# Pooled attention and a GELU layer on one core: the first batch in pairs, the loads in another order

## The chip, the cores and the metric

The kernel runs on one core of one Trainium2 chip. The metric is the device time of one execution in microseconds. One execution was also profiled; its span runs from the first to the last instruction that the profile shows, and its own time is a little longer than that.

A core has five engines that run side by side, each through its own list of instructions in order: PE (matmuls and transposes, with PEld for its weight loads), DVE (VectorE), ACT (ScalarE), POOL (GpSimd) and SP, which here only issues DMAs. DMAs are issued from the queues of SP, ACT and POOL and carried by 16 DMA engines. PE writes its results to PSUM, which has eight banks of 512 fp32 numbers for each of 128 partitions.

## The reference

Eight batches of 576 tokens go through attention over pooled keys and values (eight heads of 64), and then all 4608 tokens through two dense layers with a GELU (tanh form) between them.

```python
batch, n_heads, seq, head_dim = (8, 8, 576, 64)
Sp = S // 8                                     # 72 pooled positions
k_p = k.reshape(B, H, Sp, 8, D).mean(axis=3)
v_p = v.reshape(B, H, Sp, 8, D).mean(axis=3)
scores = scale * np.matmul(q, k_p.transpose(0, 1, 3, 2))
attn = softmax(scores)
attn_out = np.matmul(attn, v_p)
x = attn_out.transpose(0, 2, 1, 3).reshape(B * S, H * D)     # 4608 x 512
h = x @ w_in                                    # 512 -> 2048
g = gelu_tanh(h)
out = g @ w_out                                 # 2048 -> 512
```

All inputs and the output are fp32 in HBM.

## The kernel before

The 4608 tokens are worked through in nine groups of 512 (`for g in range(NG)`). A group runs the first layer (16 blocks `fo` of 128 features, four matmuls `ko` each, line 282), a GELU of each block on ACT (line 288), and the second layer (four row blocks, 16 matmuls each, line 291). The attention of batch g + 1 is interleaved by hand with group g. In the first layer, after the GELU of the blocks that the table `plan` names, stand the sums that pool k and v (`k_steps`, `v_steps`, on DVE) and the transposes of k and q on PE. Between the matmuls of the second layer, at the places in `pos`, stand for each of eight units (half a sequence `c`, a pair of heads `pr`): QK (line 211), Exp (line 218), AV (line 231) with the row sums beside it, Ln and Exp for the reciprocal (lines 244 to 249), and the multiply into `xT` (line 257). The order on every engine is the order in which the program issues it (`manual_schedule`); the framework only adds the waits.

Batch 0 has no group before it, so its attention stands alone at the start. Its k is loaded in two halves by SP and ACT, with the last 64 rows behind ACT's half; its v on SP's queue in four parts; its q in two halves on POOL's queue, behind which stand w_in in four column blocks of 512, batch 1's k and q, and w_out in four row blocks. DMAs on POOL's queue also change fp32 into bf16. k is summed on DVE in three adds, transposed into one PSUM bank (line 172), and copied out of it by DVE for the even heads and by ACT for the odd ones (line 178). Idle matmuls (`spin`, line 312) stand where PE would otherwise wait. Batch 0's eight units of scores come first, then v's sums, then eight times AV, Ln, Exp and the multiply, one unit at a time, with 16 of the first layer's matmuls for the first 288 tokens put between the last units. Batch 1's v is loaded by SP's queue after the fourth of these units: a memset on DVE (line 344) holds the load back until then.

What sets the order of batch 0's later units:

```python
for i, (c, pr) in enumerate(ORDER):
    bank = (4, 6, 0, 2, 4, 6, 4, 6)[i]
    av(0, c, pr, bank)
    norm(0, c, pr, bank)
    mult(0, c, pr, bank)
    if i == 3:
        vs[1] = kvp.tile([Sp, H, 512], F32, name="vt")
        nc.vector.memset(vs[1][:, 0, 0:1], 0.0)
        load_v(1, nc.sync)
```

and what of batch 1 stands in group 0's first layer:

```python
plan = {0: kk, 4: tk, 6: tq[:1], 7: tq[1:2], 8: tq[2:3], 9: tq[3:], 10: v0, 12: v1}
```

In group 0's second layer the first 32 matmuls take both of two row blocks through four features at a time, so that a quarter of w_out is needed every eight matmuls. `load_q`, `load_k` and `load_v` of batch g + 2 are issued at the start of group g, q's transpose by DMA among them.

Of the kernel before, what the change touches and what calls it, by code (L numbers as in the profile page):

```python
# [8 lines left out]
F32 = mybir.dt.float32  # L9
# [9 lines left out]
def kernel(  # L19
# [9 lines left out]
    nc = tc.nc  # L29
# [35 lines left out]
    def load_k(b, engs):  # L65
        rows = k[b].rearrange("h (j l) d -> (h j) (l d)", l=8)
        main = rows[0:128 * KR].rearrange("(p r) c -> p r c", r=KR)
        n = KR // len(engs)
        for i, eng in enumerate(engs):
            eng.dma_start(out=kts[b % 2][:, i * n:(i + 1) * n], in_=main[:, i * n:(i + 1) * n])  # L70
        engs[-1].dma_start(out=kts[b % 2][64:128, KR], in_=rows[128 * KR:])

    def load_v(b, eng, h0=0, h1=H):
        if b not in vs:
            vs[b] = kvp.tile([Sp, H, 512], F32, name="vt")
        rows = v[b, h0:h1].rearrange("h (j l) d -> j h (l d)", l=8)

        for j0, j1 in ((0, 64), (64, Sp)) if eng is nc.sync else ((0, Sp),):
            eng.dma_start(out=vs[b][j0:j1, h0:h1], in_=rows[j0:j1])
# [8 lines left out]
    w_in_b = consts.tile([128, KO, DF], BF16, name="w_in_b")  # L88
    w_out_b = consts.tile([128, FO, DM], BF16, name="w_out_b")
    w_in_v = moe_w_in.rearrange("(ko p) f -> p ko f", p=128)  # L90
    w_out_v = moe_w_out.rearrange("(fo p) d -> p fo d", p=128)
# [4 lines left out]
    load_v(0, nc.sync, 0, 4)  # L96
    load_v(0, nc.sync, 4, 8)
# [4 lines left out]
    def load_w_in(i):  # L102
        nc.gpsimd.dma_start(out=w_in_b[:, :, i * 512:(i + 1) * 512], in_=w_in_v[:, :, i * 512:(i + 1) * 512])  # L103

    load_w_in(0)
    load_w_in(1)
# [21 lines left out]
    nc.gpsimd.memset(kTs[1], 0.0)  # L128
    nc.gpsimd.memset(kps[1], 0.0)
    nc.gpsimd.memset(kts[1][0:64, KR], 0.0)  # L130
    nc.gpsimd.memset(vps[0], 8.0)  # L131
    nc.gpsimd.memset(vps[1], 8.0)  # L132

    load_k(1, [nc.gpsimd])
    load_q(1)
    load_w_in(2)
    load_w_in(3)
    for i in range(4):
        nc.gpsimd.dma_start(out=w_out_b[:, 4 * i:4 * i + 4, :], in_=w_out_v[:, 4 * i:4 * i + 4, :])

# [3 lines left out]
    def add(o, a, b):  # L144
        nc.vector.tensor_tensor(out=o, in0=a, in1=b, op=ALU.add)  # L145

    def k_steps(b):

        t = kts[b % 2]
        return [lambda: add(t[:, :, 0:256], t[:, :, 0:256], t[:, :, 256:512]),  # L150
                lambda: add(t[:, :, 0:128], t[:, :, 0:128], t[:, :, 128:256]),
                lambda: add(kps[b % 2][:, 0:KR + 1], t[:, :, 0:64], t[:, :, 64:128])]
# [15 lines left out]
    def trans_k(b, bank, odd_eng=None):  # L168
        tp = half_bank(bank)[:, 0:(KR + 1) * 128].rearrange("p (r c) -> p r c", c=128)
        kf = kps[b % 2].rearrange("p r d -> p (r d)")  # L170
        for r in range(KR + 1):
            nc.tensor.transpose(out=tp[:, r, :], in_=kf[:, r * D:r * D + 128], identity=identb)  # L172
        tp = tp[0:D]
        n7 = (H - 1) * KH
        for e in range(2):
            copy = nc.scalar.copy if e and odd_eng is nc.scalar else nc.vector.tensor_copy
            o = kTs[b % 2][e * 64:(e + 1) * 64, e]
            copy(out=o[:, 0:H - 1].rearrange("p h (j r) -> p h j r", r=KR),  # L178
                 in_=tp[:, 0:KR, 0:n7].rearrange("p r (h j) -> p h j r", j=KH))
            copy(out=o[:, H - 1, 0:(128 - n7) * KR].rearrange("p (j r) -> p j r", r=KR),  # L180
                 in_=tp[:, 0:KR, n7:128].rearrange("p r j -> p j r"))
            copy(out=o[:, H - 1, (128 - n7) * KR:], in_=tp[:, KR, 64:128])

    def trans_q(b, i, t0, n, bank, eng):
        if b not in qTs:
            qTs[b] = bp.tile([128, 2, TP, 128], BF16, name="qT")
        tp = half_bank(bank)[:, 0:n * 128].rearrange("p (t c) -> p t c", c=128)
        for x in range(n):
            nc.tensor.transpose(out=half_bank(bank)[:, x * 128:(x + 1) * 128],
                                in_=qs[b][:, i, (t0 + x) * 128:(t0 + x + 1) * 128],  # L190
                                identity=identb)
        o = qTs[b][:, i, t0:t0 + n]
        if eng is nc.scalar:
            nc.scalar.copy(out=o, in_=tp)
        else:
            nc.vector.tensor_copy(out=o, in_=tp)

# [43 lines left out]
    def norm(b, c, pr, bank):  # L241
        ld = ep.tile([128, CH], F32, name="ld")
        if b:
            nc.scalar.activation(out=ld[0:64], in_=PS[64:128, bank, :CH], func=ACT.Ln)  # L244
            nc.scalar.activation(out=ld[64:128], in_=PS[0:64, bank + 1, :CH], func=ACT.Ln)  # L245
        else:
            nc.scalar.activation(out=ld, in_=PS[:, bank + 1, :CH], func=ACT.Ln)
        rc = ep.tile([128, CH], F32, name="rc")
        nc.scalar.activation(out=rc, in_=ld, func=ACT.Exp, scale=-1.0)  # L249
        rcs[b, c, pr] = rc  # L250

    def mult(b, c, pr, bank):
        rc = rcs.pop((b, c, pr))
        col = b * S + c * CH
        for x in range(2 if b else 1):
            rows = slice(x * 64, (x + 1) * 64) if b else slice(0, 128)
            nc.vector.tensor_tensor(out=xT[rows, pr, col:col + CH], in0=PS[rows, bank + x, :CH],  # L257
                                    in1=rc[rows], op=ALU.mult)

# [20 lines left out]
    def p1_mm(g, fo, ko, c0=0, c1=GROUP):  # L280
        r0 = g * GROUP
        nc.tensor.matmul(out=PS[:, h_bank(g, fo), c0:c1], lhsT=w_in_b[:, ko, fo * 128:(fo + 1) * 128],  # L282
                         rhs=xT[:, ko, r0 + c0:r0 + c1], start=(ko == 0), stop=(ko == KO - 1))
# [20 lines left out]

    act_set(EXP_SET)
    for s in k_steps(0):
        s()

    def spin(n):

        for _ in range(n):
            nc.tensor.matmul(out=PS[:, 7, :], lhsT=idle[:, 0:128], rhs=idle, start=True, stop=True)  # L312

    def scores(b, c, pr, bank):
        qk(b, c, pr, bank)
        expo(b, c, pr, bank)

    spin(16)
    trans_q(0, *QG[0], 5, nc.scalar)
    trans_q(0, *QG[1], 6, nc.scalar)  # L320
    spin(4)
    trans_k(0, 4, nc.scalar)
    trans_q(0, *QG[2], 5, nc.vector)
    trans_q(0, *QG[3], 6, nc.vector)
    spin(2)
    for i, (c, pr) in enumerate(((0, 0), (0, 1), (1, 0), (1, 1), (0, 2), (0, 3), (1, 2), (1, 3))):
        if i:
            spin(1)
        scores(0, c, pr, (2, 0)[i % 2])
    for hf in range(2):  # L330
        for s in v_steps(0, hf):
            s()

    early = [(fo, ko) for ko in range(KO) for fo in range(4)]
    take = (0, 0, 0, 0, 0, 4, 6, 6)
    for i, (c, pr) in enumerate(ORDER):
        bank = (4, 6, 0, 2, 4, 6, 4, 6)[i]
        av(0, c, pr, bank)
        norm(0, c, pr, bank)
        mult(0, c, pr, bank)  # L340
        if i == 3:

            vs[1] = kvp.tile([Sp, H, 512], F32, name="vt")
            nc.vector.memset(vs[1][:, 0, 0:1], 0.0)
            load_v(1, nc.sync)
        for fo, ko in early[:take[i]]:
            p1_mm(0, fo, ko, 0, CH)
        early = early[take[i]:]


    for g in range(NG):
        nb = g + 1 if g + 1 < B else None
        act_set(GELU_SET)
        if g + 2 < B:

            load_q(g + 2)
            trans_q_dma(g + 2)
            nc.gpsimd.tensor_copy(out=gate, in_=qTs[g + 2][0:1, 1, TP - 1, 0:2])  # L358
            load_k(g + 2, [nc.gpsimd])
            load_v(g + 2, nc.gpsimd)  # L360


        side = {fo: [] for fo in range(FO)}
        if nb is not None:
            kk = k_steps(nb)
            v0, v1 = v_steps(nb, 0), v_steps(nb, 1)
            tk = [lambda: trans_k(nb, 4)]
            if g:
                plan = {2: kk[:1], 3: kk[1:], 7: v0[:1], 8: v0[1:], 9: tk, 11: v1[:1], 12: v1[1:]}
            else:  # L370
                tq = [lambda a=a, i=i: trans_q(nb, *a, 4 + i, nc.vector) for i, a in enumerate(QG)]
                plan = {0: kk, 4: tk, 6: tq[:1], 7: tq[1:2], 8: tq[2:3], 9: tq[3:], 10: v0, 12: v1}
            for fo, what in plan.items():
                side[fo] += what
# [3 lines left out]
        if g == 0:  # L378
            first = [(fo, ko, CH) for ko in range(KO) for fo in range(4)]
        else:  # L380
            late = 3
            rest = [fo for fo in range(4) if fo != late]
            first = [(fo, ko, 0) for ko in range(2) for fo in rest]
            first += [(late, 0, 0), (late, 1, 0)]
            first += [(fo, ko, 0) for ko in (2, 3) for fo in rest + [late]]
        for fo, ko, c0 in first:
            p1_mm(g, fo, ko, c0)
        for fo in range(FO):
# [4 lines left out]
            for s in side[fo]:  # L393
                s()

# [63 lines left out]
```

The softmax here doesn't subtract the row's maximum and nothing guards it: scores larger than these inputs give would overflow.

## Time and profile before

| | us |
|---|---|
| median of 3 runs | 312.05 (310.88 to 312.41) |
| the profiled execution | 311.66 |
| its span | 309.9 |
| PE busy | 296.7 (96% of the span) |
| ACT busy | 220.9 (71%) |
| DVE busy | 157.1 (51%) |
| POOL busy | 30.8 (10%) |

Busy times are sums over the span and PE's include idle matmuls. The profile also has the span in 40 slices of 7.75 us, the chain of waits that ended last, groups of instructions with the mean time of one, a timeline, and the DMA queues with their packets; each can be asked for a stretch of time. "idle before <-releaser" is the time that an engine stood still ahead of an instruction, and what ended it.

### The profile page before, as it was taken

The numbers are of one execution on the slowest core, as the hardware profiler recorded it, in microseconds if no ns is written. First come the engines' busy times: TensorE is split into PE (matmuls) and PEld (weight loads), VectorE is DVE, ScalarE is ACT, GpSimd is POOL, SyncE is SP. The second block draws the span as 40 slices with busy tenths as digits, with TensorE's granted clock in tenths as the row PEclk, the third lists the DMA queues.
The fourth block names the chain that finished last, engine by engine and source line by source line (L and its number), as shares of the span: only waits on it lengthen the run. The fifth ranks groups of instructions, "written<-read, shape, count | busy, mean of one in ns | idle before, by whom it ended". The sixth has DMA issues, their size and how long they took to land.

```text
span 309.9 us, 4249 instructions
## 1 busy us (share of the span) xinstructions
PE 296.7 (96%) x1516; PEld 149.5 (48%) x1545; DVE 157.1 (51%) x304; ACT 220.9 (71%) x414; POOL 30.8 (10%) x54
## 2 busy tenths in 40 slices
PE   7788899999999999999999999999999999999994
PEld 2455455444544455445544554455445544444441
DVE  3867536647568455855495358636772640020011
ACT  1597478877997799778987898689868987306500
POOL 8530000300301200030003000200000000000000
PEclk9999999999999999999999999999999999999999
DMA  7999995894895982588358826572101120121022
GB/s 225 232 279 249 178 200 116 266 225 87 258 224 113 237 186 62 112 225 175 85 110 232 185 68 100 166 182 68 41 0 33 49 56 0 36 68 34 2 68 69
DMA packets 32701, 41.05 MB, mean 132 GB/s; under 512 B 17608, under 2 KB 21704, under 8 KB 31784
## 3 DMA queue, kind: packets, MB, share of 16 engines
q0 software_dynamic: 10160, 24.26, 35.4%
q1 hardware_dynamic: 22200, 15.74, 21.8%
q10 hardware_dynamic: 320, 0.79, 0.8%
q8 instruction: 12, 0.20, 0.3%
q14 instruction: 9, 0.07, 0.1%
HBM read 36.70 MB, written 9.44 MB: 149 GB/s over the span
## 4 chain that ended last, share of the span: by engine, by line
PE 83%; DMA 12%; POOL 2%; issue 1%; ACT 0%; DVE 0%; POOLq 0%
PE PS L291 38%; PE PS L282 36%; DMA w_out_b<-in_moe_w_out_dram 8%; DMA kt<-in_k_dram 4%; PE PS L211 4%; PE PS L231 4%; PE PS L172 1%; POOL w_in_b L103 0%; POOL kT L128 0%; POOL qb L84 0%; POOL vp L131 0%; POOL vp L132 0%; DVE osb L296 0%; ACT e L218 0%; POOL kt L130 0%
## 5 line engine op out<-in xcount | busy, mean ns | idle before, releaser
L291 PE MATMUL PS<-w_out_b,gT 128*128 128x512 bf16 x560 | 133.8, 379 | 0.9
L282 PE MATMUL PS<-xT,w_in_b 128*128 128x512 bf16 (+2 forms) x580 | 128.3, 373 | 1.8 <-DMA w_in_b<-in_moe_w_in_dram 0.9
L288 ACT ACTIVATE gT<-PS 128x512 bf16<-128x512 f32 x144 | 81.3, 603 | 48.4 <-PE PS L282 48.2
L282 PEld LDWEIGHTS <-w_in_b 128*128 128x128 bf16 x592 | 57.2, 98 | 66.4 <-issue 2.0
L291 PEld LDWEIGHTS <-gT 128*128 128x128 bf16 x576 | 56.0, 97 | 57.1 <-issue 0.8
L296 DVE COPY osb<-PS 128x512 f32<-128x512 f32 x36 | 24.9, 692 | 94.9 <-PE PS L291 94.9
L257 DVE TENSOR_TENSOR xT<-PS,rc 64x288 bf16<-64x288 f32 (+1 forms) x120 | 54.6, 455 | 29.9 <-ACT rc L249 22.3
L218 ACT ACTIVATE e<-PS 72x576 bf16<-72x576 f32 x64 | 40.7, 644 | 8.4 <-PE PS L211 7.6
L145 DVE TENSOR_TENSOR vt<-vt 72x1024 f32<-72x1024 f32 (+1 forms) x32 | 30.5, 952 | 7.0 <-DMA vt<-in_v_dram 6.2
L249 ACT ACTIVATE rc<-ld 128x288 f32<-128x288 f32 x64 | 28.3, 443 | 2.1
L211 PE MATMUL PS<-qT,kT 128*72 128x288 bf16 x128 | 26.1, 286 | 0.4 <-ACT e L218 0.3
L244 ACT ACTIVATE ld<-PS 64x288 f32<-64x288 f32 x56 | 22.8, 408 | 1.4
L245 ACT ACTIVATE ld<-PS 64x288 f32<-64x288 f32 x56 | 22.5, 402 | 1.4
L263 ACT ACT_TABLE_LOAD x17 | 21.8, 1283 | 2.1 <-issue 1.8
L231 PE MATMUL PS<-e,vp 72*128 72x288 bf16 x112 | 23.1, 285 | 0.0
L211 PEld LDWEIGHTS <-kT 128*72 128x72 bf16 x128 | 14.4, 113 | 14.2 <-issue 1.4
L145 DVE TENSOR_TENSOR kt<-kt 128x1280 f32<-128x1280 f32 (+1 forms) x16 | 18.5, 1158 | 4.7 <-DMA kt<-in_k_dram 4.3
L358 POOL COPY gate<-qT 1x2 bf16<-1x2 bf16 x6 | 1.1, 176 | 155.8 <-DMA qT<-qb 155.8
L178 DVE COPY kT<-PS 64x504 bf16<-64x504 bf16 x15 | 10.1, 675 | 7.1 <-PE PS L172 7.0
L231 PEld LDWEIGHTS <-vp 72*128 72x128 bf16 x112 | 11.0, 98 | 3.3
L312 PE MATMUL PS<-idle 128*128 128x512 bf16 x28 | 9.6, 467 | 1.2 <-DVE idle L120 1.2
L145 DVE TENSOR_TENSOR vp<-vt 72x128 bf16<-72x128 f32 x28 | 6.9, 284 | 0.6
(45 smaller groups left out, 75.5 us busy)
## 6 DMA issues: line engine op xcount, KB each, us to landing
out_dram<-osb SPq DMA_DIRECT2D x142, 64.0 KB, 1.7
kt<-in_k_dram POOLq DMA_DIRECT2D x7, 1024.0 KB, 5.8
vt<-in_v_dram POOLq DMA_DIRECT2D x6, 1152.0 KB, 12.4
qb<-in_q_dram POOLq DMA_DIRECT2D x7, 576.0 KB, 15.1
w_in_b<-in_moe_w_in_dram POOLq DMA_DIRECT2D x4, 512.0 KB, 18.4
w_out_b<-in_moe_w_out_dram POOLq DMA_DIRECT2D x4, 512.0 KB, 25.0
vt<-in_v_dram SPq DMA_DIRECT2D x2, 512.0 KB, 11.1
vt<-in_v_dram SPq DMA_DIRECT2D x1, 1024.0 KB, 11.6
```

What stands on the lines that cost most here:

```text
L145: nc.vector.tensor_tensor(out=o, in0=a, in1=b, op=ALU.add)
L211: nc.tensor.matmul(out=PS[:Sp, bank + e, :CH].rearrange("j (t p) -> j t p", p=32), lhsT=kTs[b % 2][:, c, h, :], rhs=qTs[b][:, h // 4, :, h ...
L218: nc.scalar.activation(out=e, in_=PS[:Sp, bank:bank + 2, :CH], func=ACT.Exp, scale=1.0 / 64.0)
L231: nc.tensor.matmul(out=PS[:, bank + x, :CH], lhsT=flat(vps[b % 2][:, pr, x]), rhs=e[:, x, :], start=True, stop=True)
L244: nc.scalar.activation(out=ld[0:64], in_=PS[64:128, bank, :CH], func=ACT.Ln)
L245: nc.scalar.activation(out=ld[64:128], in_=PS[0:64, bank + 1, :CH], func=ACT.Ln)
L249: nc.scalar.activation(out=rc, in_=ld, func=ACT.Exp, scale=-1.0)
L257: nc.vector.tensor_tensor(out=xT[rows, pr, col:col + CH], in0=PS[rows, bank + x, :CH], in1=rc[rows], op=ALU.mult)
L282: nc.tensor.matmul(out=PS[:, h_bank(g, fo), c0:c1], lhsT=w_in_b[:, ko, fo * 128:(fo + 1) * 128], rhs=xT[:, ko, r0 + c0:r0 + c1], start=(ko ...
L288: nc.scalar.activation(out=gTs[g][:, fo, :], in_=PS[:, h_bank(g, fo), :], func=ACT.Gelu_apprx_tanh)
L291: nc.tensor.matmul(out=PS[:, o_bank(g, r), :], lhsT=gTs[g][:, fo, r * 128:(r + 1) * 128], rhs=w_out_b[:, fo, :], start=(fo == 0), stop=(fo ...
L296: nc.vector.tensor_copy(out=osb, in_=PS[:, o_bank(g, r), :])
```

## The change

- k of batch 0: the 64 last rows are loaded first. Two of the five row blocks are summed by GpSimd, three by DVE. The transposes are done twice, into banks 4 and 7; DVE copies the even heads from the one and the odd heads from the other.
- q's transposes come after k's, the first half copied by ACT and DVE; the second half follows the first two units of scores, with the first add of v ahead of its copies on DVE.
- AV, Ln, Exp and the multiply of batch 0 work on two pairs of heads at a time, in four banks: 576 columns in one instruction. Eight whole matmuls of the first layer (two of four `ko`, 512 columns) stand ahead of the last set, where 16 of 288 columns stood in several places.
- Weights: w_in is loaded in two blocks of 1024 columns, w_out in four blocks in which each partition reads four neighbouring rows. For that the features are dealt to blocks with a step of four, and the first layer's weights are read with that step in all nine groups.
- The order on POOL's queue: q of batch 0, w_in's first half; then, behind GpSimd's adds, batch 1's k, w_in's second half, batch 1's q, w_out. Batch 1's v is loaded by SP after batch 1's k was summed on DVE, in group 0's first layer, with its last eight rows first. In group 0 the transposes of q and the sums of v stand later in `plan`, and the loads of batch 2 are issued behind the first layer.

The core of the diff:

```diff
+        engs[-1].dma_start(out=kts[b % 2][64:128, KR], in_=rows[128 * KR:])
         for i, eng in enumerate(engs):
             eng.dma_start(out=kts[b % 2][:, i * n:(i + 1) * n], in_=main[:, i * n:(i + 1) * n])
-        engs[-1].dma_start(out=kts[b % 2][64:128, KR], in_=rows[128 * KR:])
...
+    BY_HALF = ((64, Sp, 0, H), (0, 64, 0, 4), (0, 64, 4, H))
+    WHOLE = ((64, Sp, 0, H), (0, 64, 0, H))
...
-    w_out_v = moe_w_out.rearrange("(fo p) d -> p fo d", p=128)
+    w_out_v = moe_w_out.rearrange("(q p j) d -> p q (j d)", p=128, j=4)
...
-        nc.gpsimd.dma_start(out=w_in_b[:, :, i * 512:(i + 1) * 512], in_=w_in_v[:, :, i * 512:(i + 1) * 512])
+        nc.gpsimd.dma_start(out=w_in_b[i], in_=w_in_v[:, :, i * 1024:(i + 1) * 1024])
...
+    def norm0(c, pr, bank):
+        ld = ep.tile([128, 2, CH], F32, name="ld0", bufs=1)
+        nc.scalar.activation(out=ld, in_=PS[:, bank + 1:bank + 4:2, :CH], func=ACT.Ln)
+        rc = ep.tile([128, 2, CH], F32, name="rc0")
+        nc.scalar.activation(out=rc, in_=ld, func=ACT.Exp, scale=-1.0)
+        nc.vector.tensor_tensor(out=xT[:, pr:pr + 2, c * CH:(c + 1) * CH], in0=PS[:, bank:bank + 3:2, :CH],
+                                in1=rc, op=ALU.mult)
...
-        nc.tensor.matmul(out=PS[:, h_bank(g, fo), c0:c1], lhsT=w_in_b[:, ko, fo * 128:(fo + 1) * 128],
+        q, j = divmod(fo % 8, 4)
+        nc.tensor.matmul(out=PS[:, h_bank(g, fo), c0:c1], lhsT=w_in_b[fo // 8][:, ko, q * 512 + j:(q + 1) * 512:4],
                          rhs=xT[:, ko, r0 + c0:r0 + c1], start=(ko == 0), stop=(ko == KO - 1))
...
+    spin(16, 1)
+    for s in k_steps(0, slice(3, KR + 1), nc.gpsimd) + k_steps(0, slice(0, 3)):
         s()
+    nc.gpsimd.memset(kps[1], 0.0)
+    nc.gpsimd.memset(kts[1][0:64, KR], 0.0)
+    load_k(1, [nc.gpsimd])
+    load_w_in(1)
+    load_q(1)
+    nc.gpsimd.memset(kTs[1], 0.0)
+    nc.gpsimd.memset(vps[0], 8.0)
+    nc.gpsimd.memset(vps[1], 8.0)
+    for i in range(4):
+        nc.gpsimd.dma_start(out=w_out_b[:, 4 * i:4 * i + 4, :].rearrange("p j d -> p (j d)"), in_=w_out_v[:, i])
...
+    va, vb = v_steps(0, 0), v_steps(0, 1)
+    trans_k_mm(0, 4)
+    trans_k_copy(0, 0, 4)
+    trans_k_mm(0, 7)
+    trans_q_mm(0, *QG[0], 5)
+    trans_q_copy(0, *QG[0], 5, nc.scalar)
+    trans_q_mm(0, *QG[1], 6)
+    trans_q_copy(0, *QG[1], 6, nc.vector)
+    trans_k_copy(0, 1, 7)
+    spin(2, 1)
+    scores(0, 0, 2)
+    scores(0, 1, 0)
+    va[0]()
+    spin(1, 7)
+    for x in (2, 3):
+        trans_q_mm(0, *QG[x], 3 + x)
+        trans_q_copy(0, *QG[x], 3 + x, nc.vector)
+    for i, (c, pr) in enumerate(((1, 0), (1, 1), (0, 2), (0, 3), (1, 2), (1, 3))):
+        spin(1, 7)
+        scores(c, pr, (2, 0)[i % 2])
+    for s in va[1:] + vb:
+        s()
+    early = [(fo, ko) for ko in range(2) for fo in range(4)]
+    av0(0, 0, 4)
+    norm0(0, 0, 4)
+    av0(1, 0, 0)
+    norm0(1, 0, 0)
+    av0(0, 2, 4)
+    norm0(0, 2, 4)
+    for fo, ko in early:
+        p1_mm(0, fo, ko)
+    av0(1, 2, 4)
+    norm0(1, 2, 4)
...
-                plan = {0: kk, 4: tk, 6: tq[:1], 7: tq[1:2], 8: tq[2:3], 9: tq[3:], 10: v0, 12: v1}
+                def load_v1():
+                    vs[1] = kvp.tile([Sp, H, 512], F32, name="vt")
+                    nc.vector.memset(vs[1][:, 0, 0:1], 0.0)
+                    load_v(1, nc.sync, WHOLE)
+                plan = {0: kk + [load_v1], 5: tk, 10: tq[:1], 11: tq[1:2], 12: tq[2:3], 13: tq[3:] + v0, 14: v1}
...
+        if g == 0:
+            load_next()
```

## The prediction

> **What bounds the kernel now.** I read the page's slices and chain first, then the windows by stage, then the timeline and the DMA view of the first 60 us.
>
> ```profile
> PE   7788899999999999999999999999999999999994
> PEclk9999999999999999999999999999999999999999
> PE 83%; DMA 12%; POOL 2%; issue 1%; ACT 0%; DVE 0%; POOLq 0%
> ```
>
> Only the first six slices (46 us) have a PE below 9; the chain's DMA and POOL share lies there too. The windows say how much (columns: stretch, its length, busy time of PE, PEld, DVE, ACT, POOL, clock, DMA share, GB/s):
>
> ```profile
> 16.50:25.60 9.10, 8.02 (x66) 6.11 (x65) 6.68 (x14) 8.33 (x19) 2.92 (x4) 1.00 1.13 276
> 25.60:40.00 14.40, 12.31 (x73) 5.97 (x73) 9.71 (x20) 8.54 (x16) 0.00 (x0) 1.00 1.28 211
> 40.00:58.50 18.50, 18.25 (x96) 9.67 (x97) 7.98 (x17) 16.12 (x32) 2.94 (x5) 1.00 0.83 166
> 58.50:90.60 32.10, 31.92 (x163) 16.11 (x165) 19.34 (x37) 26.60 (x51) 2.92 (x5) 1.00 0.81 213
> ```
>
> From 58.5 us on, a group takes 32.1 us of which PE works 31.9: that part, 251 us long, can't move unless matmuls get dearer. So the change is worth what it shifts the start of group 1's first matmul (58.49). Before it PE has 2.1 us idle in 25.6 to 40, 1.1 in 16.5 to 25.6, and the start. DMA is full all that time. The marks that I use:
>
> ```profile
> 16.54 1.94 DVE L145 TENSOR_TENSOR vt<-vt 72x1024 f32<-72x1024 f32 x2 [1.27 <-DMA vt<-in_v_dram]
> 21.12 0.06 DVE L344 MEMSET vt<- 72x1 f32 x1
> 25.65 2.55 ACT L288 ACTIVATE gT<-PS 128x512 bf16<-128x512 f32 x5
> 27.73 0.44 PE L172 MATMUL PS<-identb,kp 128*128 128x128 bf16 x5 [0.96 <-DVE kp L145]
> 35.52 1.94 DVE L145 TENSOR_TENSOR vt<-vt 72x1024 f32<-72x1024 f32 x2 [0.58 <-DMA vt<-in_v_dram]
> 36.57 3.63 PE L282 MATMUL PS<-xT,w_in_b 128*128 128x512 bf16 x16 [0.43 <-DMA w_in_b<-in_moe_w_in_dram]
> 43.54 0.41 PE L231 MATMUL PS<-e,vp 72*128 72x288 bf16 x2
> ```
>
> Batch 1's v is asked for behind the memset at 21.12 and is there at 35.5; its first use on PE is the AV at 43.54. Last, how two DMA queues share the engines (queue: packets, MB, share), in the windows 6 to 9, 26 to 31, 36 to 42 and 18.4 to 20 us:
>
> ```profile
> q0 software_dynamic: 191, 0.40, 70.0%
> q1 hardware_dynamic: 188, 0.39, 38.1%
> ...
> q1 hardware_dynamic: 427, 0.87, 63.8%
> q0 software_dynamic: 425, 0.42, 49.4%
> ...
> q0 software_dynamic: 1239, 1.24, 124.3%
> ...
> q0 software_dynamic: 86, 0.68, 100.3%
> ```
>
> First pair: GpSimd's q packets (2304 bytes written, 4608 read) beside v's of 2048: one for one. Second: w_in's (1024 written, 2048 read) beside v's: one for one again. So queues take turns by packet, whatever its size. Per engine a pair costs 3 x 16/190 = 0.253 us in the first case and 5 x 16/426 = 0.188 in the second; a lone w_in packet 6 x 16/1239 = 0.078, a lone 8192-byte packet of k 1.6 x 16/86 = 0.298. Per byte read these are the same (2048 in 0.078, 8192 in 0.298, 4% apart).
>
> **The change part by part.**
>
> *Longer runs.* w_in reads 4096 bytes a packet, w_out 8192. By that 4% the 8.4 MB of weights, 9.9 us for each matrix, gain 0.8 us at most. But a packet of w_out now costs about 0.298 in the turns, and v's packet 0.188 - 0.078 = 0.110.
>
> *First k.* DVE's adds cost 1.49, 0.82 and 0.49 (1280, 640, 320 elements): 1.04 ns each and 0.16. Three fifths of it: 0.96 + 0.56 + 0.36 = 1.88 instead of 2.80. No row shows GpSimd adding; DVE's rate bounds its 512, 256 and 128 from below (1.4), its memset (1152 in 1.08) times three streams from above (2.9). I take the upper end, as the memset is GpSimd's own row: k ready at 7.25 + 2.9 = 10.1, as before. GpSimd now issues batch 1's k and all behind it about 2.5 us later (8.14 before); the 2 MB of w_in queued ahead (5 us) cover that; uncovered it would cost those 2.5. Two transposed banks take ACT's copy off and let the first scores start at about 11.8, against 12.46.
> [...]
>
> *First v.* Its second half lands at 16.5 now. Beside w_in's packets of 4096 read (0.155 by the row above) its last 240 packets, 15 an engine, each wait 0.077 longer: 16.5 to 17.7. DVE's adds (1.22 + 0.69 + 2 x 0.28 = 2.46) then hold the first multiply until 19.0 to 20.2. The copies of q's second half now stand behind v's first add on DVE, and an idle matmul ahead of those transposes waits for the second k bank's copies (12.3); the late scores queue behind both, inside the same time.
>
> *Normalization by pairs.* Ln and Exp on 576 elements: 0.65 and 0.70 (0.395 and 0.443 for 288, 0.644 for a 576 Exp), eight instructions instead of sixteen, ACT 1.3 us shorter. But sets 3 and 4 use the same four banks, so they run one after another: AV 8 x 0.122 = 0.98, Ln 0.65, Exp 0.70, multiply 0.76: 3.1 each. First multiply done 19.8 to 21.0, so the last 26.0 to 27.2 (24.8 before). Then five matmuls to the first GELU: 27.3 to 28.5 against 25.65. PE ends the first four blocks at 27.7 to 28.9; 48 matmuls (10.4) and 23 transposes (1.4) follow. The waits of 0.96 for kp and 0.5 + 0.4 for w_in go, as k's adds end at 28.8 to 30.0 before PE asks, and w_in's second half is queued ahead of q. Second layer: 39.5 to 40.7, against 40.0. Level, then.
>
> *Batch 1's v.* This decides. Its load is now behind k's adds on DVE: SP issues at 29.0 to 30.1, not 21.2. Before, the first packet of v appeared at 25.0, 3.8 us after issue; so 32 to 34. w_in's second half (5 us) now precedes q, so w_out's packets start at about 29.3 instead of 38; of 32 an engine, 23 to 16 are left when v joins. Turn about, 0.298 + 0.110 = 0.408 a pair: 6.5 to 9.4 us, w_out done at about 41. v has 36 an engine; 13 to 20 remain, beside the next q at 0.253: 3.3 to 5.1. So 44.7 to 45.6, one microsecond to land, and up to 2.7 for a late engine (before: 36 x 0.188 from 25.0 gives 31.8 + 1, DVE got it at 35.5): 45.7 to 49.3. DVE's first-half adds 2.46: the first AV can run at 48.2 to 51.8. PE comes to it at 39.5 to 40.7 plus 14 x 0.216 and two QKs of 0.245: 43.0 to 44.2. Queued behind that AV are all second-layer matmuls, behind DVE's adds the multiplies and the output copies. The second half's adds are covered by 3.5 us of PE work. AV before: 43.54; shift 4.7 to 8.2, middle 6.5. Nothing later gives it back, as PE is full from there.
>
> *Clock.* PE would stand 4 to 8 us. The longest gap after the start is 2.0 (6.9 to 8.9), without a loss. At the start 16 idle matmuls take 5.7 us, 0.43 each for the first 4.3, then 0.21. So a restart costs 0 to 2.1; I take 1.
> [...]
>
> *Weights read with a step of four.* No row has such a load. A load takes 98 ns and has a matmul of 216 to hide under; below nothing it can't go, as it is hidden already. Loads are back to back at 0.056 in the transposes; four times that is 0.224: 576 x 8 ns = 4.6 us at worst. I take nothing: nearest are the plain rows.
>
> *The rest.* k's tail first, load_next behind the first layer: SP's and POOL's order stays (v, then transpose; w_out, then q); no cost.
>
> Sum: 6.5 + 1 = 7.5 on the profiled execution's 311.66 (span 309.9 and 1.8 around it; the median is 312.05): 319.2.
>
> **The rivals.**
> *Sharing by bytes* (not slower). If queues split bytes evenly, v takes 1.18 MB at half of 410 GB/s, 5.8 us: there at 39 to 41, adds done by 43.4, no wait. Then second layer 39.5 to 40.7, matmul 24 of it 46.2 to 47.4 against 46.7 now, where w_out's last part lands; that is 311.2 to 312.3. Six steps of the pair chain are 576 wide, which no row has for Ln and the multiply; 0.15 less for each and the first scores' 0.6 make the lower end 309.7. It decides if v lands before 41. Against it: 191 to 188 and 427 to 425.
> *Weights read slowly*: the waits as in the forecast and 4.6 more: 323.8; decides above 0.216 a load.
> *A short wait*: v joins at once (first packet 0.7 us after issue, as k's first) and no late engine: v at 43 to 44, AV at 46: +2.5 to +3, 314 to 315.
>
> **How the numbers follow.** Forecast 0.69 (316.4 to 322); sharing by bytes, or another way in which v is on time, 0.20; short wait 0.07; slow weights 0.04. Range 311.0 to 322.5: it takes in most of the first rival. 0.5% is 1.56 us, about what this kernel's measurement tells apart: faster needs below 310.5. Of the 0.20, 0.11 goes there and 0.09 to no change; the rest, 0.80, is slower. The forecast's own range is 316.4 to 322.
>
> **What would show it.** Right: DVE's first add on vt of batch 1 waits on DMA until 45 to 50, PE's line of AV waits on DVE vp for 4 to 8 us, granted clock below 1 after it, and 32.1 us a group later. Wrong: vt there before 41; or matmuls of the first layer over 0.22 apart in every group; or GELU starting before 25.

## The result: 3.1% slower, and the profile after

The changed kernel takes 321.69 us (median of 4 runs, 320.88 to 322.41), the kernel before 312.06 on the same chip: a ratio of 1.0315 [1.0278, 1.0352]. The profiled execution took 321.68, with a span of 319.9.

The page's slices of the changed kernel, with its chain of waits:

```profile
PE   7098799999999999999999999999999999999994
PEclk9788799999999999999999999999999999999999
PE 89%; DMA 3%; ACT 3%; DVE 2%; issue 1%; ACTq 0%; DVEq 0%
```

The whole difference lies in the first five slices (40 us): a slice in which PE has nothing to do, and granted clocks below full. The windows of the changed kernel (length, busy time of PE, PEld, DVE, ACT, POOL, clock, DMA share, GB/s); the last is a later group:

```profile
16.50:25.60 9.10, 8.93 (x66) 6.32 (x65) 7.47 (x17) 6.12 (x11) 8.68 (x14) 0.87 1.05 267
25.60:40.00 14.40, 10.58 (x40) 4.99 (x39) 5.75 (x8) 8.24 (x13) 0.00 (x0) 0.76 1.08 213
69.34:101.46 32.12, 31.95 (x164) 17.09 (x166) 19.26 (x38) 26.61 (x50) 2.90 (x5) 1.00 0.63 149
```

In 25.6 to 40 us PE works 10.6 us where it worked 12.3, at a mean clock of 0.76. A later group takes 32.1 us, as before: with the weights read in steps of four nothing there got dearer. The marks, from the timelines of DVE, POOL, PE and ACT:

```profile
12.57 2.49 DVE L134 TENSOR_TENSOR kt<-kt 128x768 f32<-128x768 f32 x2 [9.13 <-DMA kt<-in_k_dram]
12.64 3.00 POOL L134 TENSOR_TENSOR kt<-kt 128x512 f32<-128x512 f32 x2 [8.87 <-DMA kt<-in_k_dram]
15.91 1.35 PE L161 MATMUL PS<-identb,kp 128*128 128x128 bf16 x10 [9.09 <-DVE kp L134]
34.38 0.76 DVE L264 TENSOR_TENSOR xT<-PS,rc 128x576 bf16<-128x576 f32 x1 [3.99 <-ACT rc L263]
36.76 2.06 ACT L296 ACTIVATE gT<-PS 128x512 bf16<-128x512 f32 x4 [1.12 <-PE PS L290]
50.81 1.95 DVE L134 TENSOR_TENSOR vt<-vt 72x1024 f32<-72x1024 f32 x2 [1.60 <-DMA vt<-in_v_dram]
53.75 0.41 PE L232 MATMUL PS<-e,vp 72*128 72x288 bf16 x2
```

The first and the fourth of these in the kernel before:

```profile
7.25 2.35 DVE L145 TENSOR_TENSOR kt<-kt 128x1280 f32<-128x1280 f32 x2 [3.81 <-DMA kt<-in_k_dram]
24.34 0.46 DVE L257 TENSOR_TENSOR xT<-PS,rc 128x288 bf16<-128x288 f32 x1 [0.85 <-ACT rc L249]
```

k's adds wait for k until 12.57; before they began at 7.25. PE stands for 9 us ahead of k's transposes. The last multiply of the first batch starts at 34.38 (24.34 before), the first GELU at 36.76 (25.65). Batch 1's v lands at 50.8, later than forecast, but PE comes to its AV (the product with vp, the pooled v) only at 53.75 and waits for nothing there. From the table load ahead of the first GELU on (24.33 before, 34.36 after) the two kernels keep the same distance: group 0 takes 35.1 and 35.0 us. So the 10 us are lost before the first GELU, in the part that the prediction had called level.

The queues of the changed kernel in 6 to 9 us, the window in which the prediction shows 191 and 188 packets (386 in all, 263 GB/s):

```profile
DMA packets 190, 0.54 MB, mean 180 GB/s; under 512 B 7, under 2 KB 7, under 8 KB 190
## 3 DMA queue, kind: packets, MB, share of 16 engines
q10 hardware_dynamic: 72, 0.29, 48.6%
q0 software_dynamic: 86, 0.20, 46.6%
q1 hardware_dynamic: 32, 0.06, 14.6%
```

Half the packets, and on 16 engines as busy as before (109.8% against 108.3%): a packet takes 277 ns of an engine in the mean, 135 before. ACT's queue (q10) is still bringing its half of k, which in the kernel before was in by then (7 packets left).

### The profile page after: what moved, and what is told of

The parts are those of the page before. It is cut to its first block, busy times and chain, and to the rows that moved or that the text cites. A ratio compares the mean times of both kernels' runs of the same rounds, so it can differ in the third digit from the quotient of the medians.

```text
span 319.9 us, 4200 instructions
## 1 busy us (share of the span) xinstructions
PE 299.7 (94%) x1501; PEld 158.7 (50%) x1530; DVE 158.2 (49%) x304; ACT 219.1 (68%) x402; POOL 31.7 (10%) x55
## 4 chain that ended last, share of the span: by engine, by line
PE 89%; DMA 3%; ACT 3%; DVE 2%; issue 1%; ACTq 0%; DVEq 0%
PE PS L290 39%; PE PS L299 38%; PE PS L212 5%; PE PS L232 4%; DMA kt<-in_k_dram 3%; PE PS L161 1%; ACT e L219 1%; PE PS L237 1%; DVE kt L134 1%; ACT rc L263 1%; ACT ld L261 1%; PE PS L181 1%; DVE xT L264 0%; PE PS L316 0%; DVE osb L304 0%
## 5 line engine op out<-in xcount | busy, mean ns | idle before, releaser
L290 PE MATMUL PS<-xT,w_in_b 128*128 128x512 bf16 x564 | 130.4, 385 | 3.3 <-DVE xT L264 2.5
L290 PEld LDWEIGHTS <-w_in_b 128*128 128x128 bf16 x576 | 65.0, 114 | 62.0 <-issue 7.3
L255 DVE TENSOR_TENSOR xT<-PS,rc 64x288 bf16<-64x288 f32 x112 | 51.0, 455 | 22.3 <-ACT rc L247 20.0
L247 ACT ACTIVATE rc<-ld 128x288 f32<-128x288 f32 x56 | 24.8, 443 | 1.8
L134 DVE TENSOR_TENSOR kt<-kt 128x1280 f32<-128x1280 f32 (+3 forms) x16 | 18.7, 1167 | 9.6 <-DMA kt<-in_k_dram 9.1
L168 DVE COPY kT<-PS 64x504 bf16<-64x504 bf16 x16 | 10.8, 675 | 11.0 <-PE PS L161 10.8
L161 PE MATMUL PS<-identb,kp 128*128 128x128 bf16 x45 | 4.4, 239 | 9.1 <-DVE kp L134 9.1
L191 ACT COPY qT<-PS 128x640 bf16<-128x640 bf16 x1 | 0.7, 692 | 14.6 <-PE PS L181 14.6
```

What stands on the lines that cost most here:

```text
L134: eng.tensor_tensor(out=o, in0=a, in1=b, op=ALU.add)
```

## The experiments

Times are set against runs of the kernel before on the same chip (medians 311.2 to 312.1).

**What makes k late.** Two loads were put first: k's last 64 rows ahead of ACT's half of k, and v's last eight rows ahead of v's halves. Each alone is undone, then both; and both alone are put into the kernel before. (Batch 1's v keeps its eight rows in front in the runs on the changed kernel.)

```diff
 # k's rows last again
-        engs[-1].dma_start(out=kts[b % 2][64:128, KR], in_=rows[128 * KR:])
         for i, eng in enumerate(engs):
             ...
+        engs[-1].dma_start(out=kts[b % 2][64:128, KR], in_=rows[128 * KR:])
 # v's rows in their halves again
-    BY_HALF = ((64, Sp, 0, H), (0, 64, 0, 4), (0, 64, 4, H))
+    BY_HALF = ((0, 64, 0, 4), (64, Sp, 0, 4), (0, 64, 4, H), (64, Sp, 4, H))
```

k's rows last, expected:

> The changed kernel with one thing undone: k's last 64 rows are loaded behind ACT's half again, not ahead of it. Theory O (order of the first loads): ACT's half of k then leaves together with SP's and is there by 7 us; the last 64 rows run into the eight-row part of v, so k is whole at 8 to 10 us instead of 12.5, and the time falls by 2 to 5 us to 317 to 320. Rival B (the eight rows of v alone hold all engines up): k still at 12 to 12.5 and 321 to 322.

Measured 320.13 (318.86 to 321.71), ratio 1.0272 [1.0224, 1.032]. DVE's own blocks come in time, GpSimd's do not (DVE, POOL and PE):

```profile
6.94 1.55 DVE L134 TENSOR_TENSOR kt<-kt 128x768 f32<-128x768 f32 x2 [3.50 <-DMA kt<-in_k_dram]
9.78 2.05 POOL L134 TENSOR_TENSOR kt<-kt 128x512 f32<-128x512 f32 x2 [5.98 <-DMA kt<-in_k_dram]
12.42 1.03 PE L161 MATMUL PS<-identb,kp 128*128 128x128 bf16 x8 [3.19 <-POOL kp L134]
```

In 6 to 9 us the engines stay slow:

```profile
DMA packets 234, 0.45 MB, mean 150 GB/s; under 512 B 28, under 2 KB 28, under 8 KB 234
```

v's rows in their halves, expected:

> The changed kernel with the other thing undone: the last eight rows of batch 0's v come behind each half of v again, not ahead of it. Theory O: without the eight rows between 5 and 8 us the packets of k's second half take 160 to 250 ns instead of 500 to 700, and k is whole at 8 to 9.5 us; 316 to 319. Rival T (the place behind the last 64 rows alone makes ACT's half late): k at 11 to 12.5, 320 to 322.

Measured 320.49 (320.0 to 321.79), ratio 1.0288 [1.0252, 1.0324]. The rival's figures came out. Here the engines move 315 GB/s in 6 to 9 us, but ACT's half of k stands behind the 64 rows, in turns with q and v, and DVE's first add comes at 11.60:

```profile
DMA packets 355, 0.94 MB, mean 315 GB/s; under 512 B 14, under 2 KB 14, under 8 KB 355
11.60 2.49 DVE L134 TENSOR_TENSOR kt<-kt 128x768 f32<-128x768 f32 x2 [8.17 <-DMA kt<-in_k_dram]
```

So the slow rate goes with v's eight rows, and the late half of k with the 64 rows in front of it.

Both, expected:

> Both undone: the first loads on SP and ACT as in the kernel before, all else as changed. Theory O: k whole at 7.3 us, PE never still for more than 3 us, granted clock full from 5.4 us on, start of the first GELU table 6 to 8 us earlier than in the changed kernel. Then the forecast's other claim is tested, which the late start had covered. Theory V (batch 1's v takes turns with w_out's large packets): v there at 45 to 49 us, the first AV of batch 1 stands 3 to 6 us, 316 to 319. Rival N (v is in time): no wait of PE on batch 1's v, 311 to 314. Theory P (the pairs cost by themselves): GELU table 1.6 to 2.8 us later than before's 24.3.

Measured 317.13 (316.93 to 317.6), ratio 1.0175 [1.0148, 1.0203]. k's first add comes at 6.70, and q and v again take turns (6 to 9 us: queues; then PE):

```profile
q0 software_dynamic: 189, 0.40, 69.7%
q1 hardware_dynamic: 184, 0.38, 38.1%
10.05 1.33 PE L161 MATMUL PS<-identb,kp 128*128 128x128 bf16 x10 [2.37 <-DVE kp L134]
```

The kernel before with only these two orders, expected:

> The kernel before with only the two load orders of the change (k's last 64 rows first; the eight last rows of v first, for batch 0 and batch 1). Theory O: k whole at 11 to 12.5 us instead of 7.2, PE still for more than 3.4 us and a half clock after it; 316 to 321. Rival: the orders do it only together with the 2 MB block of w_in or another part of the change: k at 7 to 8.5, 311.5 to 313.5.

Measured 315.88 (314.75 to 317.74), ratio 1.014 [1.0087, 1.0194]:

```profile
12.08 2.35 DVE L147 TENSOR_TENSOR kt<-kt 128x1280 f32<-128x1280 f32 x2 [8.65 <-DMA kt<-in_k_dram]
```

So the orders cost some 4 us in either kernel, 4.6 of the change's 9.6, and each alone is enough to hold a part of k. The delay is larger than its cost: here the last multiply starts 5.8 us later (30.10), and group 0, whose weights are then in time, gives 1.6 back (33.5 us).

**What the late v of batch 1 costs.** With both orders undone PE is early enough to wait for it (DVE, then PE):

```profile
46.20 1.95 DVE L134 TENSOR_TENSOR vt<-vt 72x1024 f32<-72x1024 f32 x2 [4.39 <-DMA vt<-in_v_dram]
48.99 0.50 PE L232 MATMUL PS<-e,vp 72*128 72x288 bf16 x2 [2.48 <-DVE vp L134]
```

So its load was moved back to where it stood, behind the second of the four sets:

```diff
     norm0(1, 0, 0)
+    vs[1] = kvp.tile([Sp, H, 512], F32, name="vt")
+    nc.vector.memset(vs[1][:, 0, 0:1], 0.0)
+    load_v(1, nc.sync, WHOLE)
...
-                plan = {0: kk + [load_v1], 5: tk, ...
+                plan = {0: kk, 5: tk, ...
```

> The kernel after with both of k's and v's old load orders, and batch 1's v asked for behind the second multiply of the first batch, not in group 0's first layer. With both orders alone the time was 317.1, group 0 took 37.4 us, DVE got batch 1's v at 46.2 and PE waited 2.5 us for vp at its first AV. Theory (the late load, taking turns with w_out): v is there before 41, PE's wait for vp is gone, group 0 takes 34.9 to 35.1 and the time is 314.4 to 315.0. Rival (v only moves the contention: w_out or w_in comes late in its place): PE waits for a weight at about 43 to 47 instead, group 0 still over 36.5, time 316.3 to 317.5. Second rival (what group 0 lost was the clock at half speed from 27.5 to 30.9): the wait goes but under 1 us of time with it.

Measured 314.40 (312.52 to 315.26), ratio 1.0083 [1.005, 1.0116]. DVE has v in time and PE's AV waits for nothing; group 0 takes 33.3 us instead of 37.4:

```profile
40.78 1.94 DVE L134 TENSOR_TENSOR vt<-vt 72x1024 f32<-72x1024 f32 x2 [0.48 <-DMA vt<-in_v_dram]
44.84 0.41 PE L232 MATMUL PS<-e,vp 72*128 72x288 bf16 x2
```

The profiled execution gained 4.2, of which 2.5 is that wait. Most of the rest is the clock. Granted clocks changed at steps of 3.41 us (last section); windows of that length, counted on from such a change, with v late and with v early, around the wait for the last multiply (2.25 and 2.24 us long):

```profile
24.08:27.49 3.41, 1.63 (x11) 0.90 (x10) 0.78 (x2) 1.54 (x3) 0.00 (x0) 1.00 1.11 212
27.49:30.90 3.41, 2.79 (x7) 0.99 (x7) 3.28 (x5) 1.54 (x2) 0.00 (x0) 0.50 1.07 214
```

```profile
23.46:26.87 3.41, 2.01 (x13) 1.11 (x11) 0.76 (x1) 1.36 (x3) 0.00 (x0) 1.00 1.11 219
26.87:30.28 3.41, 2.26 (x10) 1.25 (x11) 3.06 (x4) 2.57 (x5) 0.00 (x0) 1.00 1.19 210
```

An edge cuts the wait in both: 1.6 us of it lie ahead of the edge in the first, 1.15 in the second, and only the first is followed by half speed. From the end of the wait to k's transposes of batch 1 it is 4.8 us in the one (28.11 to 32.92) and 3.5 in the other (27.97 to 31.42). Among the six runs with v early, two had a mean clock of 0.993 and took 312.5 and 312.8, four had 0.981 to 0.988 and took 313.8 to 315.3.

**k's adds on DVE alone**, with both orders undone:

```diff
-    for s in k_steps(0, slice(3, KR + 1), nc.gpsimd) + k_steps(0, slice(0, 3)):
+    for s in k_steps(0):
```

> The kernel after with both of k's and v's old load orders, and k's adds of the first batch on DVE alone. With both orders alone k's first add came at 6.70 and the first transpose at 10.05, and DVE's share of the adds took 2.3 + 0.76 us of work beside GpSimd's. Theory (the two engines hold each other up): DVE alone takes 1.49 + 0.82 + 0.49 = 2.8 as in the kernel before, transposes start at 9.6 to 9.8, and the time is 0 to 0.5 us less: 316.6 to 317.1. Rival (the shared adds do gain, and only the landing hid it): transposes start 0.5 us or more later than 10.05 and the time is 317.6 or more.

Measured 317.62 (317.05 to 318.53), ratio 1.0206 [1.0177, 1.0235]: not told apart from the shared adds. Transposes start 2.93 us after the first add (6.91 to 9.84), with shared adds 3.35 (6.70 to 10.05); the 0.4 us is then lost in a longer wait for v (3.06 instead of 2.48).

**What the clock costs in the changed kernel.**

```diff
-    spin(16, 1)
+    spin(56, 1)
...
     av0(1, 0, 0)
+    warm(12, 7)
...
     av0(1, 2, 4)
+    warm(20, 7)
```

(`warm` issues idle matmuls into columns 288 to 511 of a bank, which nobody reads.)

> The kernel after with 40 more idle matmuls ahead of k's transposes (PE stood from 6.8 to 15.9) and 12 and 20 short ones in the two waits of the normalization's chain, in columns that nobody reads. k lands no earlier. Theory A (the late k sets the start, the clock adds to it): the half-speed stretches of 12.1 to 18.9, 29.2 to 32.6 and 36.0 to 39.4 go or shrink; of PE's work in them 1 us lies on the path in the first, 1 in the second (8 matmuls took 2.86 instead of 1.89) and 1.7 in the third, so the time falls by 2 to 4 us, to 317.7 to 319.7. Rival B (the clock costs nothing, since PE waits for others there): 321.2 to 322.2. Rival C (PE's idle stretch itself is the loss, as the late clock makes everything behind it late): 315 or less.

Measured 320.99 (320.87 to 322.74), ratio 1.0319 [1.0291, 1.0347], at full clock throughout, and no gain, though k was in 1 us earlier by chance (11.56). The last 20 idle matmuls held the last Ln, which waited for them (ACT):

```profile
31.66 0.65 ACT L261 ACTIVATE ld<-PS 128x576 f32<-128x576 f32 x1 [3.94 <-PE PS L315]
```

Without those 20:

> The kernel after with 40 more idle matmuls ahead of k's transposes and 12 short ones in the first wait of the normalization; the 20 of the run before, which held the last Ln back by 2.1 us (it waited for them until 31.66), are left out. Theory A (the clock cost 1 to 2 us): the clock is full until 28, the first GELU table comes at 30.9 to 31.9 instead of 34.4, PE then waits about 2 us for batch 1's vp, which the lateness had hidden, and the time is 318.9 to 320.2. Rival B (all that the clock gives is given back to v): 321 to 322. Rival C (the lost clock was most of the loss): 316 or less.

Measured 319.88 (318.92 to 320.76), ratio 1.0275 [1.0246, 1.0303]. The clock stays full until 33.1, the last multiply comes at 31.62 instead of 34.38, 0.5 of that because k was in at 12.04 this time, and PE then waits 0.90 for vp. The medians differ by 1.8 from the changed kernel's, but the kernel before was 0.8 faster on this chip (311.23 against 312.06); by the ratios it is 1.2, and the intervals overlap. So a gain is not shown.

**The parts in the kernel before.** First w_in's second half ahead of batch 1's q, and k's transposes one block later:

```diff
     load_k(1, [nc.gpsimd])
-    load_q(1)
     load_w_in(2)
     load_w_in(3)
+    load_q(1)
...
-                plan = {0: kk, 4: tk, ...
+                plan = {0: kk, 5: tk, ...
```

> The kernel before with one thing of the change alone: w_in's second half is queued ahead of batch 1's q on GpSimd's queue, and batch 1's k transposes stand one block later in group 0. In the kernel before PE waited 0.96 us for kp and 0.52 and 0.43 for w_in in group 0. Theory (this part of the change was good, and was hidden under the rest): the three waits go, batch 1's q is still in time for its transposes (it needs about 5 us beside v), and the time is 1.4 to 1.9 us less: 310.1 to 310.7. Rival (the waits move: q or w_out comes late in their place): a wait for qb or w_out_b of 1 us or more shows and the time is 311.5 to 313.

Measured 315.26 (314.59 to 318.19), ratio 1.0135 [1.0102, 1.0168]. The three waits went, and a longer one came (PE):

```profile
32.73 0.45 PE L189 MATMUL PS<-identb,qb 128*128 128x128 bf16 x5 [3.66 <-DMA qb<-in_q_dram]
```

Then with the changed kernel's later places for q's transposes and v's sums as well:

```diff
+                plan = {0: kk, 5: tk, 10: tq[:1], 11: tq[1:2], 12: tq[2:3], 13: tq[3:] + v0, 14: v1}
```

> The kernel before with w_in's second half ahead of batch 1's q, as in the run that moved this alone (315.3; PE waited 3.66 us for that q), and now also with the changed kernel's places in group 0: k's transposes after block 5, q's after blocks 10 to 13, v's sums after 13 and 14. Theory (order and places belong together; with them group 0 takes the 33.3 us that it took in the run with both old load orders and an early v, against 35.1 before): GELU tables at 24.4 and 57.5 to 58.0, no wait for w_in, kp or qb over 0.3 us, time 310.0 to 310.8. Rival (the weights' short runs make w_out late when the second layer starts at 38 instead of 41): a wait for w_out_b or vp of over 1 us and 311.5 to 313.

Measured 313.06 (310.33 to 316.76, 12 runs); the ratio, without the longest run, is 1.0034 [1.0006, 1.0063]. Four runs took 310.3 to 310.9, about as expected; the others 312.8 and more. The one with a profile is the longest, and in it PE waits for q again, 4.69 us until 37.39. For the others no profile says whether q was in time; the four have a mean clock of 0.997 to 1.0, the seven 0.995, as the run above with its wait of 3.66 us.

That kernel with the weights in longer runs:

```diff
-    w_out_v = moe_w_out.rearrange("(fo p) d -> p fo d", p=128)
+    w_out_v = moe_w_out.rearrange("(q p j) d -> p q (j d)", p=128, j=4)
 # w_in in two blocks of 1024 columns, its weights read with the step of four
```

> The kernel before with the new order and places of group 0, and with the weights in longer runs, read with a step of four. Theory (longer packets of w_in hold up batch 0's v in the turns): v's second half reaches DVE at 17.5 to 18.0 instead of 16.5, the first GELU table moves from 24.4 to 25.5 to 25.9, and the time is 1.0 to 1.5 us above the same kernel with short runs. Rival (longer runs cost nothing, as the forecast has them but for v): table at 24.4 and no difference. Second rival (the step of four costs): over 2 us more, with groups longer than 32.1.

Measured 312.68 (312.29 to 313.15), ratio 1.0041 [1.0025, 1.0057]. Batch 0's v is a microsecond later, as expected (17.57; 16.5 with short runs), PE then waits for its sums, and a half-speed stretch follows (six matmuls of 288 columns take 1.64 us there, 0.90 with short runs); the last multiply is at 26.82. In exchange q of batch 1 is in time, and group 0 takes 33.4 us. The expected 1.0 to 1.5 us over short runs did not come out: it is no slower than that kernel's 313.06, and 2.2 above the four runs of 310.3 to 310.9. Batch 1's v, asked for at 22.3, lands at 42.1; in between (30 to 36 us) it takes turns with w_out:

```profile
17.57 1.94 DVE L143 TENSOR_TENSOR vt<-vt 72x1024 f32<-72x1024 f32 x2 [2.52 <-DMA vt<-in_v_dram]
q0 software_dynamic: 265, 0.96, 79.1%
q1 hardware_dynamic: 265, 0.54, 26.1%
44.53 0.50 PE L229 MATMUL PS<-e,vp 72*128 72x288 bf16 x2 [0.72 <-DVE vp L143]
```

Last, the kernel before with the new order and places and with normalization by pairs:

```diff
-    for i, (c, pr) in enumerate(ORDER):
-        bank = (4, 6, 0, 2, 4, 6, 4, 6)[i]
-        av(0, c, pr, bank)
-        norm(0, c, pr, bank)
-        mult(0, c, pr, bank)
...
+    av0(0, 0, 4)
+    norm0(0, 0, 4)
+    av0(1, 0, 0)
+    norm0(1, 0, 0)
...
```

> The kernel before with the new order and places of group 0, and with the first batch's normalization in sets of two pairs of heads (AV, Ln, Exp, multiply on 576 columns), eight whole matmuls of the first layer ahead of the last set; nothing else. Theory (sets that share banks run one after another, 3.4 us each, where single pairs overlap): the last multiply starts at 25.6 to 26.2 instead of 24.3 and the time is 1.2 to 1.8 us above the same kernel without pairs. Rival (ACT is the limit and the pairs save it 1.3 us): the same or less.

Measured 314.31 (312.89 to 315.86), ratio 1.0092 [1.0062, 1.0123], 1.25 above the kernel without pairs. That difference is no clean price of the pairs: the two intervals touch, and the kernel without them has late q in its one profile, and its four shortest times are 3.9 lower. What the pairs do to the chain is seen in the four multiplies (DVE; this profile is of the longest run):

```profile
20.39 0.76 DVE L266 TENSOR_TENSOR xT<-PS,rc 128x576 bf16<-128x576 f32 x1 [1.33 <-ACT rc L265]
21.79 0.76 DVE L266 TENSOR_TENSOR xT<-PS,rc 128x576 bf16<-128x576 f32 x1 [0.64 <-ACT rc L265]
23.82 0.76 DVE L266 TENSOR_TENSOR xT<-PS,rc 128x576 bf16<-128x576 f32 x1 [1.27 <-ACT rc L265]
28.59 0.76 DVE L266 TENSOR_TENSOR xT<-PS,rc 128x576 bf16<-128x576 f32 x1 [4.00 <-ACT rc L265]
```

The sets that share banks follow each other at 3.4 us where the clock is full; the eight matmuls ahead of the last set fell into a half-speed stretch here (3.54 us instead of 1.89), which makes it 4.8. Single pairs had their last multiply at 24.6.

No kernel of these is reliably faster than the one before.

## Why the prediction was right, and where not

The direction was right and the size near (319.2 forecast, 321.7 measured), but that is luck. The forecast rests on PE standing 4.7 to 8.2 us at batch 1's v, and in the changed kernel PE waits for nothing there (53.75). A loss of 10 us before the first GELU, in the part called level, stands in its place and covers it. Of the forecast's signs only the 32.1 us of a later group came out; v was there at 50.8 and not by 50, and the clock is 1.00 behind that AV. Point by point:

- **k's tail first, "no cost"**: the step that failed. Under *First v* the eight rows were not priced at all. The two orders cost 4.6 us (321.69 to 317.13). The prediction looked at whether SP's and POOL's order stays, and not at what now stands behind the moved parts: ACT's half of k behind the one, everything in flight beside the other. Its "k ready at 10.1" is what the kernel does with the old orders (first transpose at 10.05).
- **Batch 1's v**: the mechanism was right and is seen where nothing covers it. With the old orders the memset stands at 30.78 (SP's issue was forecast for 29.0 to 30.1), v lands at 46.2 (forecast 45.7 to 49.3) and the first AV runs at 48.99 (48.2 to 51.8). The term of 6.5 us was mis-sized, since PE came to that AV at 46.5 and not at 43 to 44; the wait is 2.5, and moving the load back gave 2.7. In the changed kernel itself PE was later still and the wait is gone. The turns by packet stand: 265 to 265 for 8192-byte and 2048-byte reads, 6 x 16/265 = 0.362 us a pair and engine, where 0.408 was put.
- **The first batch "level"**: wrong also with k in time. First scores at 12.99 (11.8 forecast, 12.46 before): the second set of transposes and the copies queue behind each other, and at a clock of 0.50 from 10.4 to 13.8 (two idle matmuls take 1.06 us there, 0.59 before). In the 3.41 us ahead of that PE was at work for 1.01 us, as q's transposes now come after k's. This costs nothing yet, as DVE then waits 1.14 us for v. v's second half comes at 17.94 (forecast up to 17.7), 1.4 later than before. A set of two pairs takes 3.4 us and not 3.1, so the last multiply starts at 27.29, 2.95 us later than before. In the kernel before, longer runs brought v 1 us later; a price of the pairs alone is not shown.
- **What the change gives**: the places in group 0 do remove the waits for kp and w_in; with v early, group 0 takes 33.3 us instead of 35.1. The prediction had named these waits but let them vanish in "level".
- **Clock, +1**: not confirmed. The term was for a restart after the stand at batch 1's v. Where PE does stand there (2.48 us, old orders) the clock stays at 1.00 behind it (the next six matmuls take 1.46 us, as in the kernel before); half speed came elsewhere, behind the late k and the waits between the sets. What idle matmuls gave back there is within the noise.
- **Weights with a step of four: nothing** held: 32.1 us a group with and without. From the second group on a load takes 113 ns instead of 98, hidden under the matmuls.
- **GpSimd's share**: the upper end (2.9 us after k lands) was too low by some 0.5: 3.35 to the first transpose, where DVE alone takes 2.93, so the share gained nothing. DVE's two larger adds took 2.49 us beside GpSimd's, 1.55 where GpSimd was still waiting; GpSimd's two took 3.00 and 2.05.

One after the other the two shares would take 1.91 + 2.50 = 4.41 us by the times without overlap (k's rows last); side by side they ended after 3.6 us (12.57 to 16.18). So they hold each other up, but do overlap; spans on GpSimd are rough.

That v's eight rows slow the first loads is shown (150 GB/s with them alone in front, 315 with the 64 rows alone, 259 with neither); why they do is not.

In sum, of the 9.6 us: 4.6 the two load orders with what the clock adds, 2.7 the late v, 2.3 the rest, in which, as far as the rows go, pairs and longer packets cost more than group 0's new places give back; no run takes it apart. The last term is a difference of medians on chips whose runs of the kernel before differ by 0.8.

## What to carry to other kernels

Price a reordered load by what stands behind it in its own queue and what is in flight beside it, above all a small one that is moved to the front because it is small. When two delays lie one behind the other, the first can hide the second: undo the first before judging the second, and expect a gain upstream to turn into a wait downstream. A resource order (which transfer goes first) and the places of its users are one change, and either alone can be a loss.

## What the runs showed of the hardware

**Granted clocks changed at steps of 3.41 us.** In the first 49 us of the changed kernel the granted clock was 0.50 from 12.09 to 18.92, from 29.16 to 32.57 and from 35.98 to 39.40, once for two such steps and twice for one, and 1.00 otherwise. A wait of 2.2 us was followed by a half-speed stretch of 3.41 us in one of the two profiles above, with 1.6 us of it ahead of the edge, and by none in the other, with 1.15. No bound of PE's busy time parts the windows cleanly: half speed followed windows with 1.63 us of it (v late) and 2.09 (the kernel before with the longer runs), and did not follow 1.46 (the kernel before, at its start) or 2.01 (v early).

**v's transfer to 64 partitions, alone, ran at 193 GB/s, k's to 128 at 416.** Batch 1's v in the changed kernel, 64 partitions with little beside it (43 to 47 us), and batch 0's k in the kernel before, 128 partitions (3 to 4.8 us), both fp32 to fp32:

```profile
DMA packets 395, 0.77 MB, mean 193 GB/s; under 512 B 21, under 2 KB 21, under 8 KB 395
q1 hardware_dynamic: 357, 0.71, 98.4%
```

```profile
DMA packets 184, 0.75 MB, mean 416 GB/s; under 512 B 1, under 2 KB 1, under 8 KB 184
q10 hardware_dynamic: 96, 0.39, 53.1%
q1 hardware_dynamic: 88, 0.36, 48.7%
```

The engines are busy all the time in both, at half the rate in the first. There v's 357 packets hold them 98% of 16 x 4 us, 176 ns each; in the turns with w_out above it is 26.1% of 16 x 6 us for 265, 95 ns each. v's packets are also smaller than k's (2 KB against 4 KB), but packets of v of the same size took 95 ns there, so the size alone does not make the 176.
